# Scores of two chunks as three float32r products of parts, with a new order of steps

## The chip, the core and the metric

The kernel runs on one core of one Trainium2 chip. What counts is the device time of one execution, in microseconds, as a median of runs. The core has a matrix engine (TensorE, PE in the profile, its weight loads PEld), VectorE (DVE), ScalarE (ACT), GpSimd (POOL) and SyncE (SP), which here issues nearly all DMAs. Each works through its own queue in order; semaphores join them.

## What is computed

Causal attention over 4 batches of 12 heads (448 positions, 64 wide), followed by a layer of eight experts in which every token goes to the expert with the highest cosine score:

```python
scores = (1 / sqrt(64)) * q @ k.T            # q, k, v: (4, 12, 448, 64), float32
attn = softmax(where(causal_mask, scores, -1e9))
x = (attn @ v) -> (1792, 768)                # 4 * 448 tokens, 12 * 64 columns
idx = argmax(normalize(x) @ normalize(expert_emb).T / tau, axis=1)     # 8 experts
out[token] = gate * (relu(x[token] @ w1[idx]) @ w2[idx])               # w1: 768 x 1024, w2: 1024 x 768
```

The routing is a decision, so the attention has to be computed to nearly float32 precision.

## The kernel before

Two heads of a batch are a pair; there are 24 pairs (`p`), six to a batch. For each pair `qk[p]` brings q and k transposed (partitions 0 to 63 head 0, 64 to 127 head 1; 2 x 448 columns, tile `raws[p % 4]` in `ak`) and `vv[p]` brings v. The 448 query rows are cut into four chunks `i` of 112; chunk `i` sees 112 (i + 1) key columns.

The steps of a pair, by their names in `ORDER`: `LD` issues the two loads on SP. `S1`, `S3`, `S02` compute scores on TensorE, the digits being chunks (two digits: both chunks into one PSUM bank for each head). Each head is a product on half of the array's rows (64), at `tile_position` (0, 0) or (64, 0), with its own bank. `Mih` (VectorE, chunk i, head h) adds the causal mask, turns the sign and takes the row's extremum (L373). `Eih` is the exponent on ScalarE, with the row's sum (L378). `Tn` transposes the result on TensorE in 112 x 112 pieces (L396), and `Vn` moves them to SBUF (L401). The groups `n` are chunk 0 of both heads ("0"), chunk 1 of both ("1"), chunk 2 of one head ("20", "21"), chunk 3 of one head ("30", "31"). A letter in `GROUPS` says which engine moves a group: ScalarE ("A") or VectorE ("V"); only "31" is VectorE's. `PV0` to `PV3` multiply with v (L409), each head on half of the array's columns. `VO` moves the result to SBUF (ScalarE, L415). `SA` adds 1e-9 to the sums on GpSimd (L416), `RC` takes the reciprocal (VectorE, L417). `X` transposes back, and `XE` scales into the token matrix (VectorE, L431). `LT`, `LS`, `LO`, `LE` compute routing logits of three pairs at a time (L446), `R0` to `Rc` the routing of a batch on VectorE, `Q0` to `Q3` the squared norms on ScalarE. `WX` writes the tokens of a batch to memory.

Towards the end the expert products begin between attention steps. `LWk` loads a slice of the first expert's w1 into one of three stages, `Wk` casts it to float32r (ScalarE, `h1[k]` in tile `wh1`), `Wlk` subtracts that from the original (GpSimd, `l1[k]` in tile `wl1`, L541), six slices each. `LLj`, `Ak`, `Bk` do the same for w2 (ScalarE and VectorE, L743). `F0` to `F5` and `G...` are expert products, each of them three float32r products of high and low parts (L657 to L659). After the list a loop goes over tiles of 128 tokens.

What is done in which order is written out by hand: `ORDER` is a list of `step.pair`, which is gone through once, each step emitting its instructions. So an engine's queue holds its instructions in the order of the list. Of a float32 matmul the trace shows two records, of a float32r matmul one.

Of the kernel before, what the change touches and what calls it, by code (L numbers as in the profile page):

```python
# [42 lines left out]
M21.3 E11.2 PV0.1 esA.0 E10.2 XE.0 PV1.1 E01.2 RC.1 E20.2 PV2.1 M00.3 M20.3 E21.2 PV3.1 T0.2 LD.5 T1.2 VO.1 V0.2 V1.2
S3.3 E30.2 S1.3 M30.3 T21.2 E00.3 SA.2 M31.3 T20.2 E01.3 V21.2 X.1 M11.3 V20.2 T30.2 M10.3 T31.2 E31.3 XE.1 V31.2 V30.2
S02.4 RC.2 E10.3 PV0.2 M01.4 E11.3 M21.4 E20.3 PV1.2 M00.4 M20.4 E21.3 PV2.2 PV3.2 E30.3 T0.3 LD.6 T1.3 VO.2 SA.3 V0.3
V1.3 S3.4 RC.3 E00.4 LT.2 M30.4 E01.4 M31.4 E20.4 LS.2 T21.3 T20.3 V21.3 X.2 V20.3 T30.3 E31.4 XE.2 T31.3 V31.3 V30.3
S1.4 S02.5 E21.4 M11.4 M10.4 E30.4 PV0.3 M01.5 M21.5 E10.4 PV1.3 M00.5 E11.4 M20.5 PV2.3 E00.5 SA.4 PV3.3 E01.5 T0.4
# [5 lines left out]
LS.5 T20.6 T30.6 V20.6 X.5 V30.6 T31.6 XE.5 E21.7 T0.7 V31.6 V0.7 S02.8 WX.5 Q0.5 S3.8 M01.8 M21.8 Q1.5 PV0.6 M00.8
M20.8 Q2.5 M30.8 PV1.6 M31.8 PV2.6 PV3.6 Q3.5 LO.5 T1.7 LE2.5 LD.10 VO.6 LE0.5 T21.7 V1.7 LE1.5 R0.5 S1.8 V21.7 S02.9
M11.8 E30.7 R1.5 R2.5 T20.7 E31.8 R3.5 SA.7 T30.7 R4.5 V20.7 M10.8 X.6 R5.5 V30.7 T31.7 R8.5 E00.8 M01.9 T31.8 R9.5
E10.8 V31.7 S3.9 E11.8 V31.8 E01.8 PV0.7 M21.9 E20.8 XE.6 PV1.7 E21.8 RC.7 RK.5 M00.9 E30.8 PV2.7 M20.9 R6.5 PV3.7 E00.9
R7.5 SA.8 T0.8 LD.11 M30.9 VO.7 T1.8 Ra.5 V0.8 Rb.5 V1.8 T21.8 Rc.5 X.7 V21.8 T20.8 M31.9 E01.9 T30.8 V20.8 S1.9 XE.7
# [932 lines left out]
```

## Time and profile before

| | us |
|---|---|
| median of 3 runs | 515.34 (515.24 to 518.18) |
| the profiled execution | 516.07 |
| its span in the trace | 514.4 |

| engine | busy us | share of the span |
|---|---|---|
| PE | 494.9 | 96% |
| PEld | 397.6 | 77% |
| ACT | 339.0 | 66% |
| DVE | 299.9 | 58% |
| POOL | 71.2 | 14% |

The span is one execution. A matmul's end is modelled, so a busy PE isn't one at its peak; distances between starts tell more. A share over the whole span mixes two stages: the attention until about 190 us, and the expert products behind it. In a row of the trace, `out<-in` are tiles by name, `x12` is the number of instructions merged, and brackets hold the idle time before them with what ended it.

### The profile page before, as it was taken

How to read it: one execution, taken by the hardware profiler on the slowest of the kernel's cores; microseconds unless marked ns; L12 is line 12 of the kernel's file. 1: busy time of each engine (PE TensorE's matmuls, PEld its weight loads, DVE VectorE, ACT ScalarE, POOL GpSimd, SP SyncE). 2: the span in 40 equal slices, each digit the busy share in tenths (PEclk: the TensorE clock that was granted, in tenths of full speed). 3: DMA queues.
4: the chain of work that ended last, by engine and by line, in shares of the span. 5: the costliest groups of instructions: out<-in, count | busy, mean ns of one | idle time of the engine just before them, and what ended most of it. 6: DMA issues, size and time to landing. Idle time of an engine off the chain costs nothing. (4 is left out here: it accounts for less than half of the span.)

```text
span 514.4 us, 10514 instructions
## 1 busy us (share of the span) xinstructions
PE 494.9 (96%) x3176; PEld 397.6 (77%) x3176; DVE 299.9 (58%) x836; ACT 339.0 (66%) x820; POOL 71.2 (14%) x90
## 2 busy tenths in 40 slices
PE   8999999999999978899999999999999999999993
PEld 5566566666666646888899898999989989998983
DVE  4766576586667659540135984546758431265871
ACT  6999999999999996231245963627666531255770
POOL 2000000000000560321120122100211020011101
PEclk9999999999999999899999999999999999999998
DMA  7223443263345850301439673478596412559541
GB/s 252 74 90 108 126 146 107 73 198 109 108 125 175 338 210 18 94 32 62 171 139 371 249 281 144 167 255 331 213 356 193 141 61 100 213 211 371 190 144 34
DMA packets 27365, 87.17 MB, mean 169 GB/s; under 512 B 2694, under 2 KB 3142, under 8 KB 27280
## 3 DMA queue, kind: packets, MB, share of 16 engines
q1 hardware_dynamic: 24160, 72.38, 40.0%
q0 software_dynamic: 3120, 13.77, 7.6%
q8 instruction: 39, 0.64, 0.5%
q14 instruction: 46, 0.38, 0.2%
HBM read 144.33 MB, written 12.58 MB: 305 GB/s over the span
## 5 line engine op out<-in xcount | busy, mean ns | idle before, releaser
L378 ACT ACTIVATE aq<-aq,mx 112x112 f32<-112x112 f32 (+3 forms) x192 | 99.7, 524 | 4.0 <-DVE mx L373 4.0
L373 DVE CUSTOM_DVE_ANT_0 aq<-bank,ar 112x112 f32<-112x112 f32 (+1 forms) x192 | 76.0, 442 | 29.9 <-PE bank L368 29.5
L396 PE MATMUL bank<-idt,aq 112*112 112x112 f32 x480 | 62.6, 265 | 1.6 <-ACT ap L401 0.8
L396 PEld LDWEIGHTS bank<-idt,aq 112*112 112x112 f32 x480 | 46.8, 133 | 19.7 <-ACT ap L401 7.0
L368 PE MATMUL bank<-ak 64*112 64x112 f32 (+3 forms) x384 | 56.2, 416 | 0.8 <-DVE mx L373 0.8
L839 DVE TENSOR_TENSOR wl<-fa,wh 128x1024 fp32r<-128x1024 f32 x42 | 48.5, 1221 | 13.4 <-PE bank L658 10.8
L682 ACT COPY fa<-bank 128x512 f32<-128x512 f32 x28 | 15.2, 588 | 58.3 <-PE bank L657 51.9
L401 ACT COPY ap<-bank 112x336 f32<-112x336 f32 (+2 forms) x120 | 51.2, 458 | 3.0 <-PE bank L396 1.1
L409 PE MATMUL bank<-ap 112*64 112x448 f32 (+3 forms) x384 | 51.2, 406 | 1.1 <-ACT ap L401 1.1
L409 PEld LDWEIGHTS bank<-ap 112*64 112x64 f32 x384 | 25.2, 136 | 31.5 <-issue 17.7
L838 ACT CAST wh<-fa 128x1024 fp32r<-128x1024 f32 x42 | 40.8, 1048 | 11.8 <-PE bank L659 9.6
L723 POOL DMA_INDIRECT out_dram<-fa,isx x18 | 24.1, 1341 | 168.5 <-ACTq L849 40.0
L378 ACT ACTIVATION_READ_ACCUMULATOR aq<-aq,mx 112x1 f32 x192 | 37.0, 193 | 0.0
L562 POOL DMA_INDIRECT fa<-xd,ig x21 | 22.4, 1066 | 105.4 <-PE bank L614 77.5
L368 PEld LDWEIGHTS bank<-ak 64*112 64x112 f32 x384 | 27.0, 173 | 12.8 <-issue 3.1
L659 PE MATMUL bank<-wh,akr 128*128 128x512 f32 x84 | 32.9, 392 | 1.3 <-DVE akr L595 1.3
L657 PE MATMUL bank<-wh,aor 128*128 128x512 f32 x84 | 32.8, 390 | 0.3 <-ACT t L885 0.3
L657 PE MATMUL bank<-wh,akr 128*128 128x512 f32 x84 | 33.0, 392 | 0.0
L659 PE MATMUL bank<-wh,apr 128*128 128x512 f32 x84 | 32.8, 391 | 0.0
L658 PE MATMUL bank<-wl,akr 128*128 128x512 f32 x84 | 32.8, 390 | 0.0
L658 PE MATMUL bank<-wl,aor 128*128 128x512 f32 x84 | 32.8, 390 | 0.0
L416 POOL TENSOR_SCALAR sum<-sum 112x8 f32<-112x8 f32 x24 | 5.6, 232 | 151.8 <-ACT aq L378 115.8
(282 smaller groups left out, 1068.3 us busy)
## 6 DMA issues: line engine op xcount, KB each, us to landing
fa<-in_w_dram SPq DMA_DIRECT2D x76, 768.0 KB
fa<-in_w_dram SPq DMA_DIRECT2D x54, 1024.0 KB
ak<-in_qk_dram SPq DMA_DIRECT2D x24, 448.0 KB
ap<-in_vv_dram SPq DMA_DIRECT2D x24, 224.0 KB
xd<-fa SPq DMA_DIRECT2D x3, 1344.0 KB
fa<-in_w_dram SPq DMA_DIRECT2D x6, 512.0 KB
xd<-fa SPq DMA_DIRECT2D x1, 1120.0 KB
fa<-xd,ig POOLq DMA_INDIRECT x21, 5.0
```

The source lines that it names most:

```text
L368: pe.matmul(o, raws[p % 4][rows, 0, CP * i : CP * i + CP], raws[p % 4][rows, 1, :n], start=True, stop=True, tile_position=(D * h, 0), skip ...
L373: v.tensor_tensor_reduce(out=Ps[p % 2][i, h], in0=st.pop(("sp", p, i, h)), in1=mask[i], scale=-0.125, scalar=3e38, op0=ALU.add, op1=ALU.mi ...
L378: ac.activation(x, x, AF.Exp, bias=mxs[p % 3][:, h, i : i + 1], scale=-1.0, accum_out=sums[p % 3][:, h, i : i + 1])
L396: pe.transpose(t[:, x, c], Ps[p % 2][i, h][:, c * CP : c * CP + CP], idt[:CP, :CP])
L401: (ac.copy if q == "A" else v.tensor_copy)(o, st.pop(("pt", p, n)))
L409: pe.matmul(bo[64 * h : 64 * h + 64, CP * c : S], vts[p % 4][:, c, 64 * h : 64 * h + 64], PTs[p % 2][:, h, 4 * c : 3 * c + NC], start=c == ...
L657: pe.matmul(acc[j], xh[:, k], wh[k][:, o], start=k == ends[0], stop=False)
L658: pe.matmul(acc[j], xh[:, k], wl[k][:, o], start=False, stop=False)
L659: pe.matmul(acc[j], xl[:, k], wh[k][:, o], start=False, stop=k == ends[1])
L723: g.indirect_dma_start(out=out, out_offset=IndirectOffsetOnAxis(ap=isx[:, t : t + 1], axis=0), in_=ob, in_offset=None, bounds_check=N - 1, ...
L838: ac.copy(h[k], r[:, k])
L839: v.tensor_tensor(l[k], r[:, k], h[k], op=ALU.subtract)
```

## The change

Five things change.

Chunks 2 and 3 no longer multiply the float32 q and k. GpSimd first copies q's rows of chunks 2 and 3 and all of k, 672 columns, to float32r (step `CQ`), then subtracts the copy from the original (step `CL`), which leaves a low part, also float32r. The scores of these chunks are then the sum of three float32r products in PSUM: high x high, high x low, low x high. Chunks 0 and 1 stay float32.

The parts lie in the last two of the six slices of `wh1` and `wl1`, two buffers used by pairs in turn, which the weight slices 4 and 5 take over later.

Group "0" (chunk 0 of both heads, 112 x 224 elements) is moved to SBUF by VectorE instead of ScalarE.

Chunk 2 shares a bank with chunk 0 as before, but is computed first (`S20` in place of `S02`).

`ORDER` is new throughout. The first pair begins with `S1`. Near the end `LW3` and `LW4` come before `LL2`, `LW5` before `LL3`, `B6` before `R6`, and `N0` before `R7`.

```diff
-GROUPS = {"0": ((0, 1), 0, "A"), "1": ((0, 1), 1, "A"), "20": ((0,), 2, "A"), "21": ((1,), 2, "A"),
+GROUPS = {"0": ((0, 1), 0, "V"), "1": ((0, 1), 1, "A"), "20": ((0,), 2, "A"), "21": ((1,), 2, "A"),
           "30": ((0,), 3, "A"), "31": ((1,), 3, "V")}
...
-        h1, l1 = ([cut(t, P, F, at=k * F) for k in range(KD)] for t in (T("wh1", [W], F32R, P), T("wl1", [W], F32R, P)))
+        w1s = [T("wh1", [W], F32R, P), T("wl1", [W], F32R, P)]
+        h1, l1 = ([cut(t, P, F, at=k * F) for k in range(KD)] for t in w1s)
+
+        QK = S // 2 + S
+        qks = [[cut(t, P, QK, at=(KD - 2) * F + i * QK) for t in w1s] for i in range(2)]
...
+        flat = [r.rearrange("p a s -> p (a s)")[:, S // 2 :] for r in raws]
+        step("CQ")(lambda p: g.tensor_copy(qks[p % 2][0], flat[p % 4]))
+        step("CL")(lambda p: g.tensor_tensor(qks[p % 2][1], flat[p % 4], qks[p % 2][0], op=ALU.subtract))
+
         def scores(p, chunks):
...
                     st["sp", p, i, h] = o = sp[h][:CP, at : at + n]
-                    pe.matmul(o, raws[p % 4][rows, 0, CP * i : CP * i + CP], raws[p % 4][rows, 1, :n],
-                              start=True, stop=True, tile_position=(D * h, 0), skip_group_check=len(chunks) > 1)
+                    if i < NC // 2:
+                        xy = [(raws[p % 4][rows, 0, CP * i : CP * i + CP], raws[p % 4][rows, 1, :n])]
+                    else:
+                        xy = [(qks[p % 2][a][rows, CP * i - S // 2 :][:, :CP], qks[p % 2][b][rows, S // 2 :][:, :n])
+                              for a, b in ((0, 0), (0, 1), (1, 0))]
+                    for z, (x, y) in enumerate(xy):
+                        pe.matmul(o, x, y, start=z == 0, stop=z == len(xy) - 1, tile_position=(D * h, 0),
+                                  skip_group_check=len(chunks) > 1)
```

Of `ORDER`, the beginning and a stretch about pairs 6 and 7, before and after:

```diff
-LD.0 LD.1 S02.0 EE.0 LD.2 S3.0 M01.0 M21.0 E01.0 M00.0 M20.0 E21.0 M30.0 S1.0 LD.3 E00.0 M31.0 E20.0 T21.0 T0.0 M11.0
+LD.0 LD.1 EE.0 CQ.0 S1.0 LD.2 M11.0 CL.0 M10.0 E11.0 E10.0 S1.1 LD.3 T1.0 M11.1 CQ.1 M10.1 V1.0 S20.0 E10.1 S3.0 CL.1
...
-T20.5 M01.7 E11.6 T30.5 M21.7 V20.5 X.4 M00.7 V30.5 M20.7 T31.5 XE.4 E10.6 T0.6 V31.5 V0.6 S3.7 E30.6 S1.7 M30.7 E00.7
-PV0.5 SA.6 M31.7 E01.7 E20.7 PV1.5 M11.7 E31.7 M10.7 PV2.5 RC.6 PV3.5 E10.7 T1.6 LD.9 VO.5 T21.6 V1.6 LT.5 V21.6 E11.7
+M21.7 V20.5 T31.5 M20.7 E10.6 T0.6 XE.4 E00.7 S3.7 V31.5 E30.6 CQ.8 S1.7 V0.6 E01.7 PV0.5 M30.7 SA.6 E20.7 M11.7 CL.8
+PV1.5 M31.7 E21.7 PV2.5 M10.7 E11.7 PV3.5 RC.6 E31.7 T1.6 LD.9 VO.5 T30.6 V1.6 S20.8 V30.6 S3.8 E10.7 M01.8 M00.8 E30.7
```

## Rows read from the trace of the kernel before

**Rows 1.** Stretches: from:to, us, busy PE PEld DVE ACT POOL, clock, DMA share, GB/s
```profile
62.50:107.50 45.00, 44.84 (x364) 28.45 (x363) 30.50 (x132) 43.95 (x145) 1.39 (x6) 1.00 0.39 124
107.50:152.60 45.10, 44.94 (x365) 28.50 (x364) 30.54 (x133) 43.82 (x144) 1.39 (x6) 1.00 0.40 124
```

**Rows 2.** Timeline (start us, us), ACT: evacuations of pairs 6 and 18
```profile
62.52 0.51 ACT L415 COPY ao<-bank 128x448 f32<-128x448 f32 x1
...
152.56 0.51 ACT L415 COPY ao<-bank 128x448 f32<-128x448 f32 x1
```

**Rows 3.** Timeline, PE: six transposes ahead of scores, then the last four of them
```profile
102.66 0.74 PE L396 MATMUL bank<-idt,aq 112*112 112x112 f32 x6
...
102.86 0.55 PE L396 MATMUL bank<-idt,aq 112*112 112x112 f32 x4
```

**Rows 4.** Timeline, PE, narrow windows: score records, first two, then of chunks 2 and 3
```profile
103.33 0.35 PE L368 MATMUL bank<-ak 64*112 64x112 f32 x2
...
103.91 0.82 PE L368 MATMUL bank<-ak 64*112 64x336 f32 x4
...
104.19 0.92 PE L368 MATMUL bank<-ak 64*112 64x448 f32 x4
...
104.56 0.54 PE L368 MATMUL bank<-ak 64*112 64x448 f32 x2
```

**Rows 5.** Timeline, PE: logits, a window of 30 ns, then the whole
```profile
100.50 0.58 PE L446 MATMUL bank<-ao,en 128*32 128x448 f32 x3
...
100.50 0.95 PE L446 MATMUL bank<-ao,en 128*32 128x448 f32 x6
```

**Rows 6.** Stretches (columns of group 1) behind the attention
```profile
185.00:195.00 10.00, 6.36 (x44) 3.48 (x42) 6.33 (x8) 10.00 (x19) 5.10 (x4) 1.00 0.36 116
195.00:205.00 10.00, 8.67 (x46) 6.69 (x45) 9.28 (x32) 6.85 (x14) 0.00 (x0) 1.00 0.09 23
```

**Rows 7.** ACT by form, 62.5 to 152.6 us (busy us, mean ns), and its timeline
```profile
L401 ACT COPY ap<-bank 112x224 f32<-112x224 f32 x12 | 4.1, 345 | 0.2
...
103.50 0.35 ACT L401 COPY ap<-bank 112x224 f32<-112x224 f32 x1
103.74 0.85 ACT L509 ACTIVATE junk<-fa 112x768 bf16<-112x768 f32 x1
```

**Rows 8.** DVE by form, 62.5 to 152.6 us
```profile
L373 DVE CUSTOM_DVE_ANT_0 aq<-bank,ar 112x224 f32<-112x224 f32 x24 | 8.5, 385 | 4.5 <-PE bank L368 4.5
...
L401 DVE COPY ap<-bank 112x448 f32<-112x448 f32 x12 | 7.2, 618 | 0.9 <-PE bank L396 0.8
```

**Rows 9.** Timeline, PE: float32r products of 384 columns
```profile
210.46 0.33 PE L657 MATMUL bank<-apr,arr 128*128 128x384 f32 x1
...
210.98 0.33 PE L657 MATMUL bank<-apr,arr 128*128 128x384 f32 x1
```

**Rows 10.** Timeline, PEld, 103.32 to 103.47 us: weight loads of the first scores
```profile
103.33 0.27 PEld L368 LDWEIGHTS bank<-ak 64*112 64x112 f32 x4
```

**Rows 11.** POOL by line (busy us, mean ns), whole span
```profile
L541 POOL TENSOR_TENSOR wl<-fa,wh 128x1024 fp32r<-128x1024 f32 x6 | 14.1, 2371 | 6.9 <-ACT wh L540 6.9
...
L241 POOL MEMSET ar<- 112x448 f32 x1 | 0.5, 466 | 0.0
```

**Rows 12.** DVE lines 373, 743 (min/median/max ns, first and last start), then POOL's timeline
```profile
L373 DVE CUSTOM_DVE_ANT_0 aq<-bank,ar x192: 210/442/626, 6.0 to 180.1; 112x112 f32<-112x112 f32 x48, 112x336 f32<-112x336 f32 x48, 112x448 f32<-112x448 f32 x48, 112x224 f32<-112x224 f32 x48
...
L743 DVE TENSOR_TENSOR aqr<-fa,akr x2: 946/2022/3099, 189.1 to 192.2; 128x768 fp32r<-128x768 f32 x2
...
174.10 7.03 POOL L541 TENSOR_TENSOR wl<-fa,wh 128x1024 fp32r<-128x1024 f32 x3 [4.53 <-ACT wh L540]
...
186.74 4.68 POOL L541 TENSOR_TENSOR wl<-fa,wh 128x1024 fp32r<-128x1024 f32 x2 [1.05 <-ACT wh L540]
```

**Rows 13.** Timeline: the first scores and the first exponent
```profile
4.83 1.77 PE L368 MATMUL bank<-ak 64*112 64x112 f32 x12
...
6.33 0.39 ACT L378 ACTIVATE aq<-aq,mx 112x112 f32<-112x112 f32 x1 [4.03 <-DVE mx L373]
```

More of the change, by code (lines that the diff above doesn't have):

```diff
@@ L43 @@
[L43 to L47, printed above, removed]
@@ L53 @@
[L53 to L57, printed above, removed]
@@ L93 @@
-V1.22 M20.23 PV1.21 W1.17 PV2.21 LL2.23 PV3.21 W2.17 LO.20 T21.22 LE2.20 VO.21 T20.22 Wl1.17 LE0.20 LE1.20 V21.22 S3.23
-V20.22 LW3.17 E30.22 S1.23 M30.23 T31.22 E00.23 M31.23 T30.22 E01.23 LL3.23 V31.22 X.21 E20.23 Wl2.17 V30.22 M11.23
-T0.23 M10.23 V0.23 XE.21 T20.23 E31.23 PV0.22 V20.23 PV1.22 W3.17 LW4.17 PV2.22 SA.22 PV3.22 RC.22 E10.23 Wl3.17 XTa.23
-VO.22 XTb.23 LW5.17 E11.23 T31.23 E21.23 X.22 V31.23 T1.23 E30.23 T21.23 XE.22 V1.23 WX1.22 SA.23 W4.17 T30.23 RC.23
-V21.23 Wl4.17 V30.23 W5.17 PV0.23 PV1.23 A1.23 PV2.23 A2.23 Wl5.17 PV3.23 B1.23 VO.23 XHa.23 B2.23 LT.23 XHb.23 XLa.23
@@ new lines @@
+M10.9 RC.8 S3.10 XE.7 E10.9 RK.5 M01.10 E11.9 M21.10 R6.5 PV0.8 E30.9 R7.5 CQ.11 Ra.5 Rb.5 PV1.8 E01.10 Rc.5 E21.10
+PV2.8 SA.9 CL.11 PV3.8 M20.10 VO.8 T1.9 LD.12 M00.10 M30.10 E00.10 T30.9 V1.9 M31.10 X.8 V30.9 T21.9 RC.9 XE.8 T20.9
+E31.10 S1.10 V21.9 S20.11 V20.9 M11.10 M10.10 E20.10 T31.9 M01.11 E10.10 M21.11 T0.10 V31.9 LT.8 E11.10 CQ.12 V0.10
+E30.10 M20.11 PV0.9 LS.8 M00.11 CL.12 E01.11 PV1.9 E00.11 PV2.9 E20.11 PV3.9 SA.10 E21.11 LO.8 LD.13 RC.10 VO.9 T1.10
+LE0.8 T30.10 LE1.8 V1.10 LE2.8 S3.11 V30.10 S1.11 M30.11 T21.10 M11.11 T20.10 V21.10 M31.11 X.9 V20.10 T31.10 M10.11
@@ new lines @@
+T30.14 R5.11 V1.14 R8.11 X.13 R9.11 V30.14 M31.15 T21.14 T0.15 E21.15 V0.15 V21.14 S20.16 E31.15 M10.15 RC.14 S3.16
+XE.13 E10.15 RK.11 M01.16 E11.15 M21.16 R6.11 PV0.14 E30.15 R7.11 CQ.17 Ra.11 Rb.11 PV1.14 E01.16 Rc.11 E21.16 CL.17
+PV2.14 PV3.14 M20.16 VO.14 T1.15 LD.18 M00.16 M30.16 E00.16 T30.15 V1.15 M31.16 X.14 SA.15 V30.15 T21.15 RC.15 XE.14
+T20.15 E31.16 S1.16 V21.15 S20.17 V20.15 M11.16 M10.16 E20.16 T31.15 M01.17 E10.16 M21.17 T0.16 V31.15 LT.14 E11.16
+CQ.18 V0.16 E30.16 M20.17 PV0.15 LS.14 M00.17 CL.18 E01.17 PV1.15 E00.17 PV2.15 E20.17 PV3.15 SA.16 E21.17 LO.14 LD.19
@@ new lines @@
+V31.21 V21.22 M11.22 E30.22 M31.22 T0.22 T20.22 LW1.17 E11.22 V0.22 PV0.21 E31.22 M10.22 PV1.21 RC.21 XE.20 E10.22
+PV2.21 LW2.17 V20.22 YP.17 SA.22 W0.17 RC.22 PV3.21 YI.17 YG.17 VO.21 T1.22 LL0.23 T30.22 V1.22 X.21 V30.22 T31.22 W1.17
+XE.21 Wl0.17 S20.23 V31.22 S3.23 M01.23 W2.17 LL1.23 M21.23 LT.20 M20.23 E01.23 M00.23 M30.23 E21.23 S1.23 Wl1.17 M31.23
+E00.23 PV0.22 LS.20 M11.23 LW3.17 E31.23 M10.23 PV1.22 E10.23 PV2.22 PV3.22 E20.23 XTa.23 Wl2.17 LW4.17 VO.22 XTb.23
+LO.20 E11.23 T0.23 E30.23 LE0.20 T21.23 V0.23 V21.23 LE1.20 LL2.23 T1.23 LE2.20 A1.23 T30.23 SA.23 X.22 V1.23 RC.23
@@ new lines @@
+V30.23 T20.23 XE.22 W3.17 T31.23 LW5.17 V31.23 V20.23 Wl3.17 W4.17 B1.23 PV0.23 LL3.23 A2.23 PV1.23 PV2.23 XHa.23 PV3.23
+B2.23 XHb.23 Wl4.17 VO.23 XLa.23 W5.17 WX1.22 XLb.23 LT.23 A3.23 X.23 LS.23 F0.23 XE.23 Wl5.17 A4.23 B3.23 A5.23 LO.23
+F1.23 B4.23 WX2.23 A6.23 LE0.23 LE1.23 A7.23 LE2.23 F2.23 R0.23 Q0.23 R1.23 R2.23 R3.23 F3.23 Q1.23 R4.23 R5.23 B5.23
+A0.23 RK.23 F4.23 B6.23 Q2.23 R6.23 N0.23 Q3.23 R7.23 F5.23 Ra.23 Rb.23 Rc.23 N1.23 N2.23 RL0.23 N3.23 N4.23 RL1.23
+N5.23 HTa.23 N6.23 N7.23 HTb.23 HHa.23 N8.23 N9.23 HHb.23 Na.23 Nb.23 Nc.23 HLa.23 TB.23 HLb.23 U0.23 U1.23 G1.23 IG.23
@@ L103 @@
+IU.23 GA.23 IS.23 U2.23 U3.23 G2.23 U4.23 U5.23 B0.23 G3.23 B7.23 G4.23 G5.23 G6.23 xta.23 xtb.23 xha.23 xhb.23 xla.23
+xlb.23
 """
-GROUPS = {"0": ((0, 1), 0, "A"), "1": ((0, 1), 1, "A"), "20": ((0,), 2, "A"), "21": ((1,), 2, "A"),
+GROUPS = {"0": ((0, 1), 0, "V"), "1": ((0, 1), 1, "A"), "20": ((0,), 2, "A"), "21": ((1,), 2, "A"),
           "30": ((0,), 3, "A"), "31": ((1,), 3, "V")}
```

90 lines of the change are left out of this document (43 added, 47 removed).

## Prediction

> **What bounds the kernel now.** The granted clock comes first: it is full over both stretches of six head pairs in the view by stretches [rows 1], so nothing of the attention stage is a matter of TensorE's clock. In the same two rows ScalarE is busy for 43.95 of 45.0 us and 43.82 of 45.1 us, VectorE for 30.5 and GpSimd for 1.4. TensorE shows 44.8 and 44.9, but its ends are modelled, so I work its load out below. The evacuation of the output (VO) starts at 62.52 us for pair 6 and at 152.56 for pair 18 [rows 2]: twelve pairs take 90.0 us, one takes 7.5.
>
> TensorE's own work for a pair, by distances between starts: 20 transposes of P at 0.096 (six of them end after 0.74, and the third starts 0.20 after the first [rows 3]; with a modelled length of 0.26 for the last, 0.48 over five steps) make 1.92 us. The scores are 112 + 224 + 336 + 448 = 1120 columns. A float32 product leaves two records for each head; the 448-column ones of both heads start at 104.19 and again at 104.56, those before them, of 336 columns, at 103.91 [rows 4]: 0.37 and 0.28 us a record, 0.83 ns a column, both heads at once. Twice 1120 columns is 1.86 us, and P times V streams the same columns, 1.86 more. Four output transposes are about 0.4, a third of the logits' 0.95 [rows 5] is 0.32. Sum 6.4 of 7.5 us. So ScalarE has about 0.17 us free in a pair, and TensorE at most 1.1, part of it changes between full array and half arrays: from the last transpose to the first score record 0.19 instead of 0.096 [rows 3, 4], so 0.09 a change, about six in a pair, 0.55 us. ScalarE bounds the stage and TensorE stands just behind it.
>
> What follows is not bounded by the scores. From 185 us on, ScalarE is full for 10 us with casts of weights, then VectorE is (9.28 of 10) with routing and splits [rows 6]. All of that, and the 300 us of expert products behind it, moves as a block if the attention ends earlier.
>
> **The change part by part.** *The evacuation of group 0 (V0) goes from ScalarE to VectorE.* One takes 345 ns [rows 7], but the next ScalarE instruction starts 0.24 us after it (103.50 to 103.74) [rows 7]. So ScalarE is relieved of 24 x 0.24 = 5.8 us; the upper bound is 24 x 0.345 = 8.3. VectorE's copy isn't in the trace at this size: above, the 448-element copy at 618 ns; below, half of that; near, its 224-element masked scores at 385 ns [rows 8]. I take 0.35: 2.1 us more in six pairs, 32.6 of about 43.5. That lies in VectorE's idle time. If that cover were gone, 8.4 us would be back on the path.
>
> *Scores of chunks 2 and 3.* Removed: for a pair and both heads 2 x (0.28 + 0.37) = 1.30 us [rows 4]. Added: three float32r products. Their rate is shown only by full-array ones: three steps from 210.46 to 210.98 for 384 columns [rows 9], 0.173 each, 0.45 ns a column. So 336 columns cost 0.151, 448 cost 0.202, and a pair 3 x 0.353 = 1.06 us if the heads still run side by side: 0.24 less, 24 x 0.24 = 5.8 us off TensorE. Three weight loads for each head instead of two: four loads of the first pair of heads end in 0.27 us with 0.17 each [rows 10], so a load follows after about 0.1, under 0.151, and stays hidden. If none were hidden, six steps a pair of 0.1 would cost 0.6 us, 14 us in all, within the prices of rivals two and three; I take nothing.
>
> Whether the heads run side by side when one head's products are issued as a row of three is the open point. For it: in the logits all three column groups start within 20 ns (three records in 0.58 us, six in 0.95 [rows 5]) although each group has two records, issued group after group. Against it: no row shows three. The Trainium skill, "TensorE: Matmul & The Clock Gate", section "Part 3: Packing small matmuls", says that matmuls start and end strictly in program order, and that only weight loads are pulled ahead. By that rule head 1 would begin when head 0's third product begins, and the change would lose TensorE time instead of saving it (rival two, by this mechanism). The trace contradicts it for rows of two records [rows 4, 5], and I weigh it down for that, not away.
>
> *CQ and CL on GpSimd.* CL is a subtraction of 672 elements in 128 partitions; the 1024-element one takes 2371 ns [rows 11], so 1.56. CQ is bounded below by a fill of 448 elements, 466 ns [rows 11], so 0.70, and above by CL's 1.56; being a one-input copy it is nearer to the fill, I take 0.9. With that, 2.5 us a pair (3.1 at most) of 7.5. S20 and S3 now wait for CL; behind a waiting S20 stand this pair's transposes and the P-times-V of the pair before, and ScalarE waits for those. What covers it: LD brings the data pairs ahead, and CL stands at least 13 steps before S20, among them all of P times V (1.86). SA queues behind CL in some pairs, RC behind SA, and masked scores behind RC on VectorE: at most 1.56 us at a time, mostly free there. I take 0.1 us in all.
>
> *The port.* While GpSimd subtracts, VectorE's masked scores don't slow: their 448-element form tops out at 626 ns [rows 12] although GpSimd was at it from 174.1 to 181.1. But one VectorE subtraction of two SBUF operands took 3099 instead of 946 ns, until GpSimd's end at 191.42 [rows 12]. In the attention stage only routing, a few operations a batch, is of that kind: from 0 to 1.56 us each time; VectorE has a third of its time free, I take 0.1.
>
> *Order at the start.* S1.0 goes first, S20.0 waits for CL.0. Data is there at 4.83, the first exponent starts at 6.33 [rows 13]; CL.0 ends at 4.83 + 0.9 + 1.56 = 7.3 (7.9 by the bound). Until then ScalarE has two 224-element exponents and V1. Loss 0 to 1 us, taken 0.1. *Order at the end.* On SP, LW3 and LW4 go before LL2, and LW5 before LL3, so LL2 and LL3 queue behind loads that wait for a free stage; A4 and A6 use them later. W4, W5, Wl4 and Wl5 overwrite the memory of the parts, which S3.23 and S20.23 have read long before. B6 goes ahead of R6: 0 to 0.95 us on VectorE's routing chain. These I take at nothing; their cover is the long wait of the expert products on other things, and without it they cost 1 us.
>
> *Sum.* ScalarE, which bounds, is relieved by 5.8; TensorE by as much, so it doesn't become the bound; losses 0.3. The profiled execution took 516.07 us (span 514.4): 516.07 - 5.5 = 510.6. The median of 515.34 is 0.73 lower, so 509.8. The stage's remaining ScalarE idle time, 1.05 us in six pairs [rows 1], is 4.2 us over 24: if the new order took all of it, 505.6.
>
> **The rivals.** *One: the time freed isn't used.* S20 and S3 wait for GpSimd, or V0 delays masked scores on VectorE, so that ScalarE waits for what it was spared. For it: VectorE goes to 75% and lies between TensorE and ScalarE twice in a pair. Against it: GpSimd is busy a third of the time. Half or more of 5.5 lost: 512 to 516, middle 513.5.
>
> *Two, slower: the heads' products no longer overlap fully.* In program order, chunk after chunk takes five steps instead of three: 5 x 0.353 = 1.77 against 1.30, plus 0.46 a pair, TensorE's work 6.87. With the changes of mode only (0.55) it is 7.42, just under 7.5; with all of today's 1.1 it is 7.97, 11 us more. Half of the waits, 7.7: plus 4.6, 520. It decides once TensorE's pair exceeds 7.5. For it: the page's rule; against it: [rows 4, 5].
>
> *Three: not at all side by side.* Six steps, 2.12, plus 0.82: 7.22 + 0.55 = 7.77 at least and 8.3 at most, 521.5 to 535, middle 528. For it only that no float32r product on half an array is in the trace.
>
> **How the numbers follow.** Forecast 0.62 (505.5 to 513 by itself), rival one 0.20, two 0.12, three 0.06. The time is the forecast's 509.8. The range from 505.5 to 517 holds the forecast, rival one and the low edge of two, 0.82. One per cent is 5.15 us, about what a measurement of this kernel can tell from no change. Faster than 510.2: two thirds of the forecast's chance, 0.43. Slower than 520.5: a little over half of rival two and all of three, 0.14. Within: 0.43.
>
> **What would show it.** Right: score records of chunks 2 and 3 in twos a few ns apart, three of them 0.15 and 0.20 us apart; six pairs in about 43.6 us; ScalarE still over 96% busy there; GpSimd at 2.5 to 3 us a pair with no wait of TensorE for it. Wrong: head 1's first record two steps after head 0's (rival two); TensorE or VectorE waiting for CL or SA, or ScalarE for V0's successors (rival one); a routing chain stretched past 1 us by GpSimd.

## The result: 0.7% slower, and the profile after

The changed kernel takes 520.31 us in the median of ten runs (517.85 to 528.14) against 515.76 for the kernel before, measured beside it. The ratio is 1.0072, with a 95% interval of 1.0051 to 1.0092: slower by 2.6 to 4.7 us. The forecast was 509.8 us, faster by 5.5. The profiled execution of the changed kernel takes 519.7 us and its span is 518.0, so it stands 3.6 us behind the profiled one of before (516.07, span 514.4).

Executions of one kernel differ by some microseconds with the clock that TensorE was granted in them (x_wlV, below: 515.05 us at a mean granted clock of 0.995, 521.35 at 0.981); so whole times are compared by medians and ratios with their intervals, and the lengths of stages are read from the profiled executions, of which there is one for each kernel.

Line numbers are 7 higher than in the kernel before ahead of the scores and 17 higher from there on: the scores are L385, the masked scores L390, exponents L395, evacuations of P's transposes L418, of the output (VO) L432, CQ and CL L367 and L368, the routing L487 to L523, the weights' subtractions Wl L558 and B L760.

The stretch of twelve pairs, from VO of pair 6 to VO of pair 18, which was 90.04 us in [rows 2], is 89.76 now (timeline of ScalarE: start us, us):

```profile
64.57 0.53 ACT L432 COPY ao<-bank 128x448 f32<-128x448 f32 x1
...
154.33 0.53 ACT L432 COPY ao<-bank 128x448 f32<-128x448 f32 x1
```

The view by stretches of the same twelve pairs (columns of [rows 1]) says what became of ScalarE's time:

```profile
64.60:109.50 44.90, 44.81 (x395) 31.28 (x394) 33.02 (x138) 42.81 (x138) 15.84 (x18) 1.00 0.42 130
109.50:154.30 44.80, 43.64 (x380) 30.92 (x380) 34.41 (x139) 41.24 (x135) 16.06 (x18) 1.00 0.38 118
```

ScalarE is busy for 42.8 and 41.2 us where [rows 1] had 43.95 and 43.82. It was relieved as planned, and the time it was spared turned into idle time. GpSimd went from 1.4 to 16 us.

The scores themselves came out as the change meant them (TensorE's timeline, one batch of chunk 2, chunk 0 and chunk 3; compare [rows 4]):

```profile
109.48 0.41 PE L385 MATMUL bank<-wh 64*112 64x336 f32 x2
109.72 0.32 PE L385 MATMUL bank<-wl,wh 64*112 64x336 f32 x2
109.87 0.32 PE L385 MATMUL bank<-wh,wl 64*112 64x336 f32 x2
110.03 0.36 PE L385 MATMUL bank<-ak 64*112 64x112 f32 x4
110.15 0.44 PE L385 MATMUL bank<-wh 64*112 64x448 f32 x2
110.43 0.37 PE L385 MATMUL bank<-wl,wh 64*112 64x448 f32 x2
110.63 0.37 PE L385 MATMUL bank<-wh,wl 64*112 64x448 f32 x2
```

Each row holds both heads (x2), although head 1's first product is issued after head 0's third. The distances are 0.15 and 0.16 us for 336 columns and 0.20 for 448, the values forecast. Only the first distance of a chunk is longer, 0.24 and 0.28. From the first score record to the last the block took 1.23 us before (103.33 to 104.56) and takes 1.15 now (109.48 to 110.63), and the last record itself 0.20 instead of 0.37: 0.25 us less in all.

Where the 3.6 us came in, by VO of the pairs 0, 6, 18 and 23 and the end of the span in both profiles: VO of pair 0 is 2.2 us late (20.33 against 18.16), the six pairs behind it take 0.1 less, the next twelve 0.3 less, the last five 0.4 less, and what follows VO of pair 23 takes 2.3 more (326.9 against 324.6). So the attention stage gained 0.8 us instead of 5.5, and the start and the end lost 4.5.

Three places show in the rows why. The first is the routing of a batch, on VectorE, GpSimd, ScalarE and TensorE (start us, us; in brackets what the engine waited for):

```profile
115.34 1.62 POOL L368 TENSOR_TENSOR wl<-ak,wh 128x672 fp32r<-128x672 f32 x1
115.89 1.11 DVE L490 TENSOR_TENSOR eq<-Lg,rmx 112x32 f32<-112x32 f32 x1
...
118.18 1.61 POOL L368 TENSOR_TENSOR wl<-ak,wh 128x672 fp32r<-128x672 f32 x1
118.41 1.40 DVE L519 TENSOR_TENSOR Os<-Os 112x8 f16<-112x8 f16 x1
119.73 0.61 DVE L390 CUSTOM_DVE_ANT_0 aq<-bank,ar 112x448 f32<-112x448 f32 x1
120.39 0.67 ACT L395 ACTIVATE aq<-aq,mx 112x448 f32<-112x448 f32 x1 [1.26 <-DVE mx L390]
120.41 0.40 PE L385 MATMUL bank<-wh 64*112 64x336 f32 x1 [1.08 <-DVE mx L390]
```

A comparison of 32 elements (L490) takes 1.11 us and an addition of 8 (L519) takes 1.40, and each ends within 0.05 us of the end of the subtraction that GpSimd began before it: 115.34 + 1.62 = 116.96, 118.18 + 1.61 = 119.79. The masked scores behind them come late, ScalarE waits 1.26 us for those and TensorE 1.08. What they take elsewhere stands in the same trace (minimum, median and maximum in ns):

```profile
L490 DVE TENSOR_TENSOR eq<-Lg,rmx x4: 192/1022/1114, 71.8 to 200.5; 112x32 f32<-112x32 f32 x4
L519 DVE TENSOR_TENSOR Os<-Os x2: 161/780/1400, 118.4 to 164.0; 112x8 f16<-112x8 f16 x2
L304 DVE TENSOR_TENSOR es<-es x3: 147/635/967, 20.8 to 23.9; 8x1 f32<-8x1 f32 x3
```

In all three batches of the attention L490 is held; the fourth, at 200.5 us, when GpSimd is idle, takes 0.19. L304 is in the square-root chain of the router's embeddings at 21 us; the evacuation behind that chain is late, and TensorE waits 1.47 us for it at 25.47.

The second place is the end. VectorE's and GpSimd's timelines, then TensorE's:

```profile
190.51 2.28 DVE L760 TENSOR_TENSOR aqr<-fa,akr 128x768 fp32r<-128x768 f32 x1 [0.75 <-ACT akr L759]
...
195.80 3.16 DVE L760 TENSOR_TENSOR apr<-fa,apr 128x768 fp32r<-128x768 f32 x1
...
188.54 9.61 POOL L558 TENSOR_TENSOR wl<-fa,wh 128x1024 fp32r<-128x1024 f32 x3 [3.58 <-ACT wh L557]
...
201.40 0.18 PE L503 MATMUL bank<-O,before 112*112 112x32 f16 x1 [2.27 <-DVE O L493]
```

GpSimd's last three weight subtractions now run until 198.15 us instead of 191.42 [rows 12], since ScalarE casts those slices later (step `Wk`). VectorE's B, 0.95 us when alone, takes 2.28 and 3.16 beside them, the last batch's routing stands behind it, and TensorE waits 2.27 us for its result. The wait is the order's doing and not that of the parts: x_order (below), with fp32 scores in this order, has the same 2.28 and 3.16 us and a wait of 2.26. Half-clock stretches follow (view by stretches, the clock is the third number from the right):

```profile
202.00:205.00 3.00, 3.00 (x9) 2.35 (x8) 2.86 (x12) 0.94 (x2) 0.00 (x0) 0.50 0.00 0
219.00:222.00 3.00, 3.00 (x8) 2.31 (x7) 2.32 (x11) 0.82 (x2) 0.00 (x0) 0.50 0.10 41
```

Each lasts 3.41 us by the record of the granted clock; the profile of before has one of them there, from 205.9 us.

The third place is the start. In the new order the score of chunk 1 of pair 1 is ahead of the first chunk-2 scores, and waits for that pair's load:

```profile
7.16 1.09 PE L385 MATMUL bank<-ak 64*112 64x224 f32 x4 [1.03 <-DMA ak<-in_qk_dram]
...
12.11 0.64 PE L385 MATMUL bank<-ak 64*112 64x224 f32 x4 [0.19 <-DVE mx L390]
```

The same four products take 1.09 us at 7.16 and 0.64 at 12.11. Up to 10.8 us TensorE's steps take about twice their later time (two chunk-2 records 0.28 us apart at 9.53, 0.15 at 13.62), as at half the clock. The record of the granted clock doesn't show it here; it reads 1.00:

```profile
7.20:10.80 3.60, 3.60 (x20) 2.71 (x22) 0.79 (x5) 2.04 (x9) 2.33 (x2) 1.00 1.03 310
```

This slow beginning goes with the order. Of the eight profiled executions whose list begins like this one, five take 0.95 to 1.09 us for those four products at 6.4 to 8 us (VO of pair 0 at 20.33 to 21.56) and three take 0.64 (18.78 to 18.94). In the ten with the beginning of before, the same four products, at 7.4 to 8.5 us, always take 0.64 (18.16 to 19.26). In x_order and x_fp7 the record shows a half clock at that place too. What brings it stays open.

### The profile page after: what moved, and what is told of

Read it like the earlier page. It is cut to its first block, busy times and chain, and to the rows that moved or that the text cites. A ratio compares the mean times of both kernels' runs of the same rounds, so it can differ in the third digit from the quotient of the medians.

```text
span 518.0 us, 10816 instructions
## 1 busy us (share of the span) xinstructions
PE 495.5 (96%) x3272; PEld 410.0 (79%) x3272; DVE 314.8 (61%) x860; ACT 332.2 (64%) x796; POOL 130.9 (25%) x138
## 5 line engine op out<-in xcount | busy, mean ns | idle before, releaser
L395 ACT ACTIVATE aq<-aq,mx 112x448 f32<-112x448 f32 (+3 forms) x192 | 99.7, 525 | 6.1 <-DVE mx L390 6.0
L390 DVE CUSTOM_DVE_ANT_0 aq<-bank,ar 112x112 f32<-112x112 f32 (+3 forms) x192 | 75.9, 444 | 34.7 <-PE bank L385 33.8
L856 DVE TENSOR_TENSOR wl<-fa,wh 128x1024 fp32r<-128x1024 f32 x42 | 48.5, 1221 | 13.5 <-PE bank L675 10.8
L418 ACT COPY ap<-bank 112x448 f32<-112x448 f32 (+1 forms) x96 | 42.9, 488 | 7.8 <-PE bank L413 7.0
L426 PEld LDWEIGHTS bank<-ap 112*64 112x64 f32 x384 | 26.4, 136 | 26.8 <-issue 15.1
L368 POOL TENSOR_TENSOR wl<-ak,wh 128x672 fp32r<-128x672 f32 x24 | 39.6, 1650 | 2.0
L395 ACT ACTIVATION_READ_ACCUMULATOR aq<-aq,mx 112x1 f32 x192 | 37.3, 194 | 0.0
L676 PE MATMUL bank<-wh,akr 128*128 128x512 f32 x84 | 33.5, 399 | 0.0
L674 PE MATMUL bank<-wh,akr 128*128 128x512 f32 x84 | 33.5, 399 | 0.0
L367 POOL CAST wh<-ak 128x672 fp32r<-128x672 f32 x24 | 18.2, 760 | 37.8 <-DMA ak<-in_qk_dram 24.8
L385 PE MATMUL bank<-ak 64*112 64x224 f32 (+1 forms) x192 | 25.6, 333 | 1.2 <-DMA ak<-in_qk_dram 1.0
```

What stands on the lines that cost most here:

```text
L368: step("CL")(lambda p: g.tensor_tensor(qks[p % 2][1], flat[p % 4], qks[p % 2][0], op=ALU.subtract))
L385: pe.matmul(o, x, y, start=z == 0, stop=z == len(xy) - 1, tile_position=(D * h, 0), skip_group_check=len(chunks) > 1)
L390: v.tensor_tensor_reduce(out=Ps[p % 2][i, h], in0=st.pop(("sp", p, i, h)), in1=mask[i], scale=-0.125, scalar=3e38, op0=ALU.add, op1=ALU.mi ...
L395: ac.activation(x, x, AF.Exp, bias=mxs[p % 3][:, h, i : i + 1], scale=-1.0, accum_out=sums[p % 3][:, h, i : i + 1])
L418: (ac.copy if q == "A" else v.tensor_copy)(o, st.pop(("pt", p, n)))
L426: pe.matmul(bo[64 * h : 64 * h + 64, CP * c : S], vts[p % 4][:, c, 64 * h : 64 * h + 64], PTs[p % 2][:, h, 4 * c : 3 * c + NC], start=c == ...
```

## The experiments

The theories were: one, GpSimd's new subtractions hold VectorE's operations wherever these have two operands in SBUF (some expectations call it the port theory); two, the new order costs; three, V0 loads VectorE and brings nothing; four, TensorE waits for the parts. All sixteen kernels were measured beside the kernel before.

### GpSimd's work, and the order without it

**x_stale** takes the later pairs' parts off GpSimd:

```diff
-step("CQ")(lambda p: g.tensor_copy(...))
+step("CQ")(lambda p: g.tensor_copy(...) if p < 2 else None)
-step("CL")(lambda p: g.tensor_tensor(...))
+step("CL")(lambda p: g.tensor_tensor(...) if p < 2 else None)
```

> The changed kernel with its order, but GpSimd makes the parts for pairs 0 and 1 alone; later pairs multiply these stale parts, so the scores of chunks 2 and 3 are of the wrong pair and the routing differs a little. TensorE's work is unchanged; 22 casts and 22 subtractions on GpSimd are gone. Theory one (GpSimd's subtraction holds VectorE's operations with two SBUF operands, which delays the square-root chain at 20 us, one routing chain at 116 to 120 us and what hangs on them, about 1.3 + 0.6 + 2.0 us of ScalarE's gaps): 515.5 to 517, and the operation at line 490 takes 0.2 us everywhere. Theory two (the new order is what costs: cold start and a TensorE-bound stretch in each batch): within 1 us of the changed kernel, 519 to 520.5. Theory four (waits for the parts themselves): 516 or less, with the score steps starting earlier.

It took 515.41 us, ratio 0.9986 (0.9962 to 1.0010), so GpSimd's work costs the changed kernel 4.9 us by the medians and 4.4 by the ratios. The twelve pairs took 88.20 us instead of 89.76, and the comparison is short in every batch:

```profile
61.80:150.00 88.20, 88.01 (x772) 61.71 (x773) 63.98 (x277) 83.96 (x274) 2.78 (x12) 1.00 0.40 127
...
L490 DVE TENSOR_TENSOR eq<-Lg,rmx x4: 191/192/193, 69.0 to 195.6; 112x32 f32<-112x32 f32 x4
```

Theory four would allow this time too, but in the changed kernel's trace all that TensorE waits for GpSimd up to 185 us is one weight load's 0.3 us. And 515.4 isn't 509.8: with the clash gone 5.6 us of the forecast are still missing; the late weight subtractions at the end are still in this kernel.

**x_order** is the kernel before with the changed order (CQ and CL struck out of it) and one letter:

```diff
-GROUPS = {"0": ((0, 1), 0, "A"), ...
+GROUPS = {"0": ((0, 1), 0, "V"), ...
```

> The kernel before with fp32 scores, but in the changed kernel's order (chunks 2 and 0 as step S20, score 1 first at the start) and with the copy V0 on VectorE; GpSimd makes no parts. Theory one (GpSimd holds VectorE): the order itself is harmless, so it lies near the kernel before, 513 to 517. Theory two (the order costs): slower than the kernel before by the start (about 2 us) and by the stretches in which TensorE is behind, which are now 0.25 us longer for each pair: 518 to 525.

520.66 us, ratio 1.0080 (1.0051 to 1.0109), as theory two had it. So order and V0 without the parts cost 4.9 us, and x_stale's parts, which save TensorE 0.25 us a pair, just give that back. Its twelve pairs took 90.80 us, with ScalarE busy for only 84.25 of them, and its rows have no wait of TensorE in them. So x_order and x_stale, which differ in the score products (and in GpSimd's work for pairs 0 and 1), compare TensorE's work alone: 2.6 us of the twelve pairs' 3.0 come out, though ScalarE had 6.5 us idle.

```profile
66.00:156.80 90.80, 90.64 (x724) 57.53 (x725) 64.15 (x277) 84.25 (x273) 2.82 (x12) 1.00 0.39 123
```

The VO rows of both, pair 0 and pair 23 of x_order, then of x_stale, divide the change by place:

```profile
21.56 0.53 ACT L415 COPY ao<-bank 128x448 f32<-128x448 f32 x1
...
193.15 0.58 ACT L415 COPY ao<-bank 128x448 f32<-128x448 f32 x1
```

```profile
18.78 0.53 ACT L432 COPY ao<-bank 128x448 f32<-128x448 f32 x1
...
186.18 0.58 ACT L432 COPY ao<-bank 128x448 f32<-128x448 f32 x1
```

From VO of pair 0 to VO of pair 23 the kernel before takes 171.56 us, x_order 171.59, x_stale 167.40 and the changed kernel 170.76. In this stage the order and V0 together cost nothing, the shorter products bring 4.2 us, and GpSimd's work takes 3.4 of them away. What the order costs lies at the start and behind VO of pair 23 (329.1 us in x_order, 324.6 before). These are single profiles.

**x_start** (kernel before's order until VO of pair 1, no parts before pair 4) and **x_tail** (kernel before's order for what is left after the step YP) join two orders:

```diff
 ORDER = """
-(the changed order)
+(x_start: before's steps up to VO.1, then the changed order's remaining ones)
+(x_tail: the changed order's steps up to YP.17, then before's remaining ones)
```

> The kernel before's order up to the output of pair 1 (about 24 us), pairs 0 to 3 with fp32 scores and GpSimd idle till then; after that the changed kernel. The changed kernel is 5.3 us behind there. If the delay of the start is carried to the end: 515 to 517. If a later wait absorbs it: 518.5 to 520.5.

> The changed kernel up to about 180 us (the step YP of the last batch's expert), from there the steps that are left in the order of the kernel before (casts and differences of the weights, the last batch's steps). If the new order of the last 15 us of the attention stage is what makes its end later: 1.5 to 3 us faster than the changed kernel, 517 to 519, the subtractions of the weights on GpSimd end by 192 us. If only the earlier delay is carried on: 520, as the changed kernel.

x_start took 517.97 us, ratio 1.0052 (1.0023 to 1.0080), and x_tail 523.08, 1.0137 (1.0106 to 1.0169). x_start lies between its two ranges, x_tail above both of its. Neither decides its question, for each made waits of its own at or behind the seam. In x_start ScalarE waits 1.97 us at 24.7, and VO of pair 2 comes 10.1 us after that of pair 1; at this seam one transposed group of pair 2 is also overwritten before its copy, so that group's values are another's. In x_tail TensorE waits 2.24 us, by this row:

```profile
189.06 0.65 PE L442 MATMUL bank<-idt,ao 128*112 128x128 f32 x4 [2.24 <-ACT ao L431]
```

### V0, the parts, and where GpSimd's subtraction lies

**x_v0A** undoes one letter in the changed kernel:

```diff
-GROUPS = {"0": ((0, 1), 0, "V"), ...
+GROUPS = {"0": ((0, 1), 0, "A"), ...
```

> The changed kernel with one word undone: V0 stays on ScalarE. If ScalarE's freed 5.8 us were used at all in the new order: 523 to 526. If in this order TensorE and VectorE's late operations set the time and the copy only filled ScalarE's gaps (16 us of them in the changed kernel): 519 to 521.5, the same as the changed kernel or faster.

518.18 us, ratio 1.0059 (1.0038 to 1.0080): the interval overlaps the changed kernel's, and there is no sign of the 5.8 us. The twelve pairs took 89.25 us instead of 89.76, with V0 back on ScalarE.

**x_parts** and **x_parts_v0** keep the order of before and put the parts into it:

```diff
 ... S3.8 CQ.9 M01.8 ... S1.8 CL.9 V21.7 S02.9 ...      (CQ and CL a pair ahead, from pair 1 on)
-                    if i < NC // 2:
+                    if i < NC // 2 or p < 1:
```

> The order of the kernel before, with the score products of parts from pair 1 on (pair 0 in fp32, so that the start is that of before), the parts made about one pair ahead by GpSimd, and V0 still on ScalarE. ScalarE keeps its 24 copies and bounds the attention stage. Theory one (GpSimd holds VectorE): slower than before by 1 to 3 us, 516.5 to 519, with long operations of the routing where GpSimd subtracts. Theory two (the order costs): 514 to 516, no slower than before, since TensorE only gains 5.5 us.

> As the run before it in this call (order of before, parts from pair 1 on), and V0 on VectorE as in the changed kernel. Theory one (GpSimd holds VectorE): 514 to 518, ScalarE gains 5.8 us and gives back 2 to 4 in waits. Theory two (the order costs): the forecast's sum comes out, 509 to 512. Theory three (V0's 24 copies load VectorE, which then is late with the masked scores): 1 us or more slower than the run without it.

With V0 on ScalarE 515.18 us, ratio 0.9978 (0.9959 to 0.9998); with V0 on VectorE 516.13, 1.0013 (0.9990 to 1.0037). The first lies where theory two had put it. The second lies where theory one had put it and 4 us above theory two's sum, so in the old order too the forecast fails; it is 0.95 us slower than the first, about what theory three said, with intervals that overlap. But the trace gives that another cause. Here the routing's operation that is held is another, the one behind which V0 stands (line 520 in these kernels, line 521 of the changed one), and ScalarE's next evacuation waits 1.15, 1.10 and 1.04 us in the three batches:

```profile
L520 DVE TENSOR_SCALAR jt<-pi x4: 170/1246/1298, 69.9 to 200.4; 112x4 int32<-112x4 int32 x4
...
72.15 0.44 ACT L417 COPY ap<-bank 112x336 f32<-112x336 f32 x1 [1.15 <-PE bank L412]
```

It has one operand in SBUF, of four elements, not two. In x_parts, where no copy stands behind it, the same operation is held for 1.26 to 1.31 us, and in the first two batches no wait as long as 0.5 us of ScalarE or TensorE follows; its twelve pairs take 88.95 us. What a hold costs depends on what stands behind it.

**x_pv0_cl** moves nothing else than GpSimd's subtraction:

```diff
-... S3.9 CQ.10 E11.8 ... SA.8 T0.8 ... S1.9 CL.10 XE.7 ...
+... S3.9 CQ.10 CL.10 E11.8 ... SA.8 T0.8 ... S1.9 XE.7 ...
```

> As x_parts_v0 (order of before, parts from pair 1 on, V0 on VectorE: 516.1 us), but GpSimd's subtraction follows its cast directly, ahead of SA instead of behind it, so that it should be over when VectorE reaches the routing's operation at line 520 and the copy V0 behind it. Port theory (the 1.25 us that line 520 takes under the subtraction, and the wait of 1.1 us that ScalarE has behind V0 in each of three batches, are what eats V0's gain): line 520 falls to about 0.17 us, 512 to 514. Rival (V0 costs because VectorE is later with everything, wherever the subtraction lies): 515.5 to 516.5.

515.04 us, ratio 0.9972 (0.9958 to 0.9987). Against 1.0013 that is 0.4%, 2.1 us by the ratios (1.1 by the medians); the time lies between the two ranges expected, but the twelve pairs went from 90.07 to 88.06 us as the port theory has it. Timelines of GpSimd and VectorE, then line 520 over the run:

```profile
66.91 1.62 POOL L367 TENSOR_TENSOR wl<-ak,wh 128x672 fp32r<-128x672 f32 x1
68.61 0.24 POOL L432 TENSOR_SCALAR sum<-sum 112x8 f32<-112x8 f32 x1
68.86 0.17 DVE L520 TENSOR_SCALAR jt<-pi 112x4 int32<-112x4 int32 x1
...
L520 DVE TENSOR_SCALAR jt<-pi x4: 164/166/171, 68.9 to 196.9; 112x4 int32<-112x4 int32 x4
```

The subtraction now ends at 68.53, before the operation starts. Same work, same engines, another place in the queue.

### The clashes in the changed kernel, one by one

**x_fp7** leaves the seven pairs that clash in fp32, **x_wlV** gives the last three weight subtractions to VectorE, **x_fp7_wlV** does both:

```diff
-                    if i < NC // 2:
+                    if i < NC // 2 or p in (4, 10, 11, 16, 17, 22, 23):
...
-lambda p, k=k: g.tensor_tensor(l1[k], stage[k % 3], h1[k], op=ALU.subtract)
+lambda p, k=k: (g if k < 3 else v).tensor_tensor(l1[k], stage[k % 3], h1[k], op=ALU.subtract)
```

> The changed kernel, but the seven pairs whose casts and subtractions meet VectorE's square-root chain, the routing or the star's chain in its trace (4, 10, 11, 16, 17, 22, 23) keep fp32 scores; GpSimd makes parts for the other 17. TensorE does 7 times 0.25 us more. Port theory: the operations at lines 304, 490, 493, 519 and 534 fall to 0.15 to 0.24 us, and 516.5 to 518.5 comes out. If it isn't the port but GpSimd's work as a whole, or the waits for the parts: 519.5 to 521.

> The changed kernel, with the last three of the six subtractions of the expert's weights (Wl3 to Wl5) on VectorE instead of GpSimd. Port theory for the tail: VectorE's subtractions at line 760, which take 1.6 to 3.2 us there, fall to 0.95; the routing of the last batch comes earlier, TensorE's wait of 2.27 us for O at 201.4 us shrinks, 516.5 to 519. If the tail is late only because the attention stage ended later: 520 to 521.5, since VectorE takes 3 us of work on.

> The changed kernel in its order, with both clashes taken out: the seven pairs in fp32 and Wl3 to Wl5 on VectorE. If the clashes are its loss: 513 to 516. If its order is (a TensorE-bound stretch in each batch, long waits in the tail, and the half-clock stretches that follow): 517 to 520.

519.32 us with the first (1.0046, 1.0020 to 1.0072) and 518.78 with the second (1.0039, 1.0007 to 1.0070): the first 0.8 us above the port theory's range and nearer to its rival's, the second inside at its upper end, and neither interval is clear of the changed kernel's. The profile of x_fp7 agrees with x_stale's all the same: from VO of pair 0 to VO of pair 23 it takes 168.28 us, 2.5 less than the changed kernel although seven pairs are in fp32; its loss lies behind (329.7 us). Together they take 516.57 us, 1.0003 (0.9977 to 1.0029), which is clear of it: 3.7 us less, from the two clashes. The time lies between the two ranges expected, so the order has its share in the rest. In x_fp7_wlV the comparison takes 0.19 us in every batch. At the end, the wait of 2.27 us for O is a wait of 0.64 in x_wlV, and after VO of pair 23 it takes 325.1 us instead of 326.9:

```profile
203.46 0.18 PE L503 MATMUL bank<-O,before 112*112 112x32 f16 x1 [0.64 <-DVE O L493]
```

In the profiled execution of x_wlV TensorE waits 1.10 us at 120.57 behind the held addition, as the changed kernel does at 120.41, and here a half clock follows:

```profile
122.00:128.00 6.00, 6.00 (x31) 3.60 (x30) 4.02 (x16) 2.89 (x12) 3.12 (x3) 0.50 0.03 7
```

Its twelve pairs took 92.53 us, against 89.76 for the same instructions in the changed kernel. In this execution half a clock came on top of the wait; that the clash brought it isn't shown.

**x_pv0_wlV** is x_pv0_cl with the same edit of the weights:

> x_pv0_cl (order of before, parts from pair 1 on, V0 on VectorE, subtraction right behind its cast: 515.0 us), with Wl3 to Wl5 on VectorE. Port theory: the subtraction at line 759 that takes 3.1 us falls to 0.95, 512.5 to 514.5. If that wait lies beside other work: 514.5 to 516.

513.20 us, ratio 0.9945 (0.9926 to 0.9964): inside the range, and faster than both kernels.

**x_pv0_fill** is x_pv0_cl with work of no use in TensorE's wait:

```diff
+            for _ in range(9):
+                pe.transpose(bank[0][:, :P], idt, idt)
             st["tb"] = cut(end_ring.next(), P, 2, NT)
```

> x_pv0_cl with nine transposes of no use on TensorE just ahead of TB, in the 1.6 us in which it waits there. If the half clock that follows at 202.7 us in x_pv0_cl comes from that idle time, it is gone and the time falls by up to 1.7 us (half of 3.41): 513 to 514. If not: 515, or 0.2 more when the transposes delay TB.

515.15 us, 0.9977 (0.9958 to 0.9995), no gain over 515.04. TensorE's wait there fell from 1.61 to 0.60 us and no half clock followed it in the profiled execution, but one of 6.83 us stood at 187.3, where x_pv0_cl has none. What a filler buys stays open.

### A square: V0 here or there, by fp32 or parts

Four kernels in the order of before, all with the weights' edit of x_wlV: x_wlV_old (fp32, V0 on ScalarE), x_wlV_fp32 (fp32, V0 on VectorE), x_wlV_v0A (parts, V0 on ScalarE) and, from above, x_pv0_wlV (parts, V0 on VectorE).

> The kernel before, with Wl3 to Wl5 on VectorE and nothing else: fp32 scores, V0 on ScalarE. The corner of the square from which the others are counted. If the clash in the tail (line 760's 3.1 us instead of 0.95) is worth what it was in x_pv0_wlV: 513 to 514.5. If not: 515 to 516.

> x_pv0_wlV (513.2 us) with V0 back on ScalarE. If the forecast's step on V0 was right (24 copies of 0.24 us more than anything else that bounds): 516 to 518.5. If with shorter score products TensorE has the room, and ScalarE bounds but V0 on VectorE costs as much in waits: 512.5 to 514.

> x_pv0_wlV with fp32 scores and no parts: order of before, V0 on VectorE, Wl3 to Wl5 on VectorE. If TensorE has no room left behind ScalarE in this order (its products' 5.5 us count once V0 is gone from ScalarE): 516 to 519. If ScalarE alone bounds: 512 to 514.

| | V0 on ScalarE | V0 on VectorE |
|---|---|---|
| fp32 | 514.31 us, 0.9965 (0.9942 to 0.9989) | 515.71 us, 0.9985 (0.9969 to 1.0002) |
| parts | 513.42 us, 0.9939 (0.9918 to 0.9961) | 513.20 us, 0.9945 (0.9926 to 0.9964) |

The twelve pairs of each, in the order x_wlV_old, x_wlV_fp32, x_wlV_v0A, x_pv0_wlV (columns as above; TensorE first, ScalarE fourth, GpSimd fifth):

```profile
63.60:153.60 90.00, 89.68 (x726) 56.85 (x724) 61.06 (x265) 87.67 (x285) 2.78 (x12) 1.00 0.39 124
```

```profile
62.30:152.70 90.40, 89.83 (x726) 56.78 (x725) 64.37 (x277) 85.39 (x273) 2.78 (x12) 1.00 0.39 123
```

```profile
62.10:150.00 87.90, 87.39 (x773) 60.63 (x772) 61.71 (x266) 86.51 (x286) 31.76 (x36) 1.00 0.40 127
```

```profile
62.30:150.50 88.20, 87.34 (x774) 60.58 (x772) 64.12 (x277) 84.80 (x274) 32.13 (x36) 1.00 0.40 126
```

Read down: the parts shorten the stretch by 2.1 and 2.2 us, 0.18 a pair, of the 0.25 that the score rows show. Read across: V0 on VectorE takes 2.3 and 1.7 us of busy time from ScalarE, and the stretch gets 0.4 and 0.3 us longer. The first is clear: x_pv0_cl, x_pv0_fill and x_pv0_wlV, which have the same instructions in this stretch, took 88.06, 88.85 and 88.19. The second lies inside that spread, so V0 on VectorE brings nothing here, rather than costs. By whole times the intervals of parts and fp32 are apart with V0 on VectorE, they overlap with V0 on ScalarE, and those of the two columns overlap in both rows. x_wlV_fp32 came between its two ranges, nearer to the one in which TensorE has no room; x_wlV_v0A came where V0 on VectorE brings nothing; its expectation put that down to waits that cost as much as ScalarE gains, and in the row of parts this isn't excluded: ScalarE is busy for 86.51 of 87.90 us in one corner, and no run relieves it without giving VectorE the copy. The corner x_wlV_old also shows that the weights' clash was in the kernel before: without it B takes 0.95 us and the kernel is faster by 0.35% (0.11 to 0.58).

## Why the prediction was wrong

The forecast was a gain of 5.8 us and losses of 0.3. In the profiles the gain was 4.2 us (x_stale against x_order), and the losses, taken at 0.1 or at nothing, were 2.2 at the start, 3.4 under GpSimd's work and 2.3 at the end. So two steps failed: what bounds the stage, which put the gain on the wrong engine, and the sizes of three losses, which make up most of the distance.

*"ScalarE bounds the stage and TensorE stands just behind it"* failed, and with it the term that was to bring the gain. I put TensorE's own work at 6.4 of 7.5 us and set its busy row of 44.84 [rows 1] aside because its ends are modelled. The square speaks against it: 2.3 and 1.7 us less on ScalarE bring nothing, and 0.25 us a pair less on TensorE bring 0.18. An engine busy for 97% of a stretch wasn't the only one that bound it.

The distances themselves show what the sum left out. When every distance between TensorE's starts in the twelve pairs of the kernel before is sorted by the kind of product (line and columns) ahead of it and behind it, the shortest of each kind add up to 84.7 of 89.9 us and the medians to 87.3: 7.1 to 7.3 us a pair, where I had 6.4, or 6.95 with the changes between full array and half arrays. The distance over the seam of two steps is longer by about 0.09, between two steps of scores too, and the small products of logits and routing (L455, L484 to L488), about 0.2 us a pair, weren't in the sum. One such seam is the last score record at 104.56 [rows 4], followed by this one after 0.47 us instead of 0.37:

```profile
105.04 0.60 PE L409 MATMUL bank<-ap 112*64 112x448 f32 x2
```

So TensorE had at most 0.2 to 0.4 us free in a pair, hardly more than ScalarE's 0.17. Taking work from ScalarE alone could bring little. When TensorE was relieved by 0.25 us a pair, the stretch followed by 0.18, about the room that ScalarE had; why V0 on VectorE opens no more room than that isn't settled.

*V0: "ScalarE is relieved of 5.8 us".* ScalarE was relieved (42.81 and 41.24 us busy), but the term for the path was 0, not 5.8. VectorE's copy takes 0.38 us (I took 0.35), and the cover, "VectorE's idle time", held for its busy time but not for its place: in x_parts_v0 it stood right behind an operation that GpSimd held, and V0's transposes keep a PSUM bank until it is done.

*The scores* held in their size: distances of 0.15 and 0.20 us, heads side by side, 0.25 us a pair. What the stage gained came from them: 4.2 us in x_stale against x_order, 0.17 a pair. Rivals two and three are out. The Trainium skill, "TensorE: Matmul & The Clock Gate", section "Part 3: Packing small matmuls", has matmuls start and end in program order; the rows at 109.48 to 110.63 contradict it for rows of three, as [rows 4, 5] did for rows of two. I was right to weigh that rule down.

*CQ and CL* cost GpSimd 0.76 and 1.65 us on average (0.9 and 1.56 taken), and one weight load waited 0.3 us for the parts themselves; that loss was sized rightly at about nothing. (Its cover was misread: CL.0 stands 11 steps before S20.0, and in most pairs only a part of P times V lies between.)

*"The port: from 0 to 1.56 us each time ... I take 0.1"* failed by 3.4 us in the stage's profiles, and by 4.4 to 4.9 in whole times (x_stale). The mechanism and the bound were in the text, from the one row of 3099 ns [rows 12], which ended at 192.24, 0.8 us behind GpSimd's end and not at it; the size was wrong by the count, and the square-root chain and L534 weren't counted at all. I took VectorE's third of free time as cover. But VectorE works in order: while a small operation is held, the masked scores behind it, which GpSimd doesn't slow, are late by as much, ScalarE starves, then TensorE. The changed kernel has ten held operations before 170 us, at L304, L490, L493, L519 and L534. The Trainium skill, "GPSIMD Engine Reference", section "8. Key points", names VectorE instructions with two SBUF inputs, and those in a 2-port mode, as the ones that contend. The trace agrees for the first (0.19 to 1.11 us at L490); the one-operand operation at line 520 (0.17 to 1.30) would be of the second kind, which no run here shows by itself.

*"Order at the start: taken 0.1"* was 2.2 us in the profiled execution. x_wlV, with the same instructions up to 170 us, had its first VO at 18.87 instead of 20.33, with the same products at 0.64 instead of 1.09 us, so 1.5 of the 2.2 is the slow rate of TensorE up to 10.8 us. That rate came in five of eight profiled executions of this beginning and in none of ten of the old one, so it counts as a price of the order, whose cause stays open; the other 0.7 lies inside the spread of the old beginning (18.16 to 19.26).

*"Order at the end: I take at nothing"* was 2.3 us. I had looked at the order of the loads and at B6 ahead of R6; what decided was that GpSimd's last weight subtractions, now 6.7 us later, moved onto VectorE's B's and so onto the last routing. With them on VectorE 1.8 us of it are gone in the profile (x_wlV). That this "moves as a block" held from there on only.

*The rivals.* Rival one ("the freed time isn't used") named the right outcome and one of its reasons: V0 brought nothing. But it ended at 516, since I had no rival in which the clash loses more than the change wins. What I named as a sign that I was wrong, "a routing chain stretched past 1 us by GpSimd", is what the trace shows in every batch of the attention.

What stays open: the price of the order as a whole. x_order against the kernel before says 4.9 us with fp32 scores, V0's move included, and its profile puts it at the start and the end; x_fp7_wlV against x_pv0_wlV says 3.4, of which seven pairs in fp32 at 0.18 are 1.3. The two runs that were to divide it by place made waits of their own.
